# Gates of the first chunk ahead of the value products, and the second chunk's weights in halves

## The chip, the cores and the metric

The kernel runs on one core of a Trainium2 chip. The time is device time in microseconds of one launch; the median of several runs counts. The profile and the trace come from one further execution, whose times are given from the start of its span. Engines are named as in the profile: PE (TensorE), DVE (VectorE), ACT (ScalarE), POOL (GpSimd), SP (SyncE, which only issues transfers).

## What is computed

A memory attention over 8 batches, 8 heads, 576 positions and 64 columns, followed by a gated feed-forward block.

```python
a = softmax(phi, axis=memory)                     # phi: 8, 8, 576, 32
k_m = einsum('bhsm,bhsd->bhmd', a, k)             # 32 memory rows per head
v_m = einsum('bhsm,bhsd->bhmd', a, v)
attn = softmax(q @ k_m.T / sqrt(64))              # 8, 8, 576, 32
x = (attn @ v_m), heads side by side              # 4608 x 512
g, val = x @ w_gate, x @ w_val                    # 512 x 1536 each
out = (silu(g) * val) @ w_out                     # 1536 x 512
```

## The kernel before

**The product that is folded.** The kernel never forms x. For each batch it multiplies the value memories with the two weight matrices first (`u_round`, products `p_u`, line 531): U = v_m x W, 256 memory rows (8 heads of 32) by 1536 columns, for the gate (`which` 0) and the value weights (`which` 1). The gate and the value of a batch then come from U and the attention weights (`gv_half`, line 592). U lives in tiles of one chunk of 512 columns (`NCH` = 3 chunks, c = 0, 1, 2) and two groups g of memory rows; one half chunk is 256 columns (`HC`).

**Slots.** A chunk of one batch has 8 slots: four blocks of 128 columns times two halves of 288 tokens. Slot s of batch b belongs to chunk s // 8, and within a chunk slots 0 to 3 need only the first half chunk. A slot is `gv_gate`: two matmuls into a bank `p_g`, and SiLU on ACT (line 609) into `t_sg`; and later a function `mul`, kept in the list `pend`: two matmuls into a bank `p_v` and one DVE multiplication (line 615) into `t_h`. `flush_mul(n)` runs the n oldest of the list; `gv_slot` does a gate and then runs what was waiting before it, so gates run one slot ahead of values.

**Copies.** Each `p_u` bank is copied, scaled by the softmax denominator, into `t_U` by ACT ("a", line 560) or DVE ("v", line 564), as the string `evac` says, group 0 first. `later` holds back the last copy of a round, so that the caller can place it further on. `u_half` makes a round of one half chunk, for the gate weights (0,), the value weights (1,) or both (0, 1); `u_item` makes a round of a whole chunk, with the gate and the value weights in banks of their own (16 matmuls of 512 columns, 4 copies).

**Banks.** There are 8 PSUM banks. `bank` takes the one at the head of the list `free`, `done` puts it at the end, both in the order of the program text: a bank comes round again after the others, and its next writer waits until its last reader is through.

**Transfers.** The inputs are cast while they are loaded, on POOL's queue, in program order. `load_w(which, c, half)` loads a weight chunk; with a half it loads 256 columns into one half of a tile laid out as [half, row block, column], else 512 columns into [row block, column]. `w_part` gives the matmul its piece of either layout. In the head of the program the order on POOL is: keys and queries of batches 0 and 1, values, then gate and value weights of chunk 0 by halves, of chunk 1 and of chunk 2 whole; then the multiplication `norm(1, 1, nc.gpsimd)` (line 512), and behind it the output weights (`load_wo`), and the keys, phi and values of batch 2. From the ninth transfer on, each issue on POOL ends a wait for an earlier transfer.

**The head.** Everything around the change is written out by hand, from `warm(104)` (matmuls on constants that fill TensorE while the first loads come in) to the last `flush_mul()` before the list `backlog`. Batches 0 and 1 are done together: attention weights first (`scores`, `z_inv`, `norm`), then the value memories of each (`v_direct`), then slots of both in turn (`g0`, `g1`), while the first half chunk, the second half chunk, chunk 1 and chunk 2 of U are made just ahead of the slots that need them. When a chunk of slots is complete, `chunk_done` lets POOL or DVE form sums of `t_h` for the output products (line 814), which follow from 54 us on. Batch 2 begins there too (`q_T`, line 438, transposes its queries on TensorE).

Of the kernel before, what the change touches and what calls it, by code (L numbers as in the profile page):

```python
# [14 lines left out]
def kernel(  # L15
# [34 lines left out]
    NCH = DF // CH  # L50
# [24 lines left out]
    def bank(shape, dtype, name):  # L75
        tag = free.pop(0)
        t = ps.tile(shape, dtype, tag=tag, name=name)
        held[id(t)] = tag, t
        return t

    def done(*tiles):

        for t in tiles:
            free.append(held.pop(id(t))[0])
# [19 lines left out]
    def load_v(b):  # L104
        t = kvs[b]
        if b in counted:
            out = t[:, NP + 1:2 * NP + 1][:, ::-1]
        else:
            out = t[:, NP:2 * NP]
        nc.gpsimd.dma_start(out=out, in_=head_pairs(v[b]))  # L110
# [32 lines left out]
    HC = CH // 2  # L143

    def load_w(which, c, half=None):

        src = (moe_w_gate, moe_w_val)[which]
        split = half is not None
        if not half:
            W[which, c] = wpool.tile(  # L150
                [128, 2, NP, HC] if split else [128, NP, CH], BF16,
                tag=f"W{which}{c}", name=f"W{which}{c}",
            )
        f0, n = (half * HC, HC) if split else (0, CH)
        nc.gpsimd.dma_start(  # L155
            out=W[which, c][:, half] if split else W[which, c],
            in_=src[:, c * CH + f0:c * CH + f0 + n].rearrange("(i p) f -> p i f", p=128),
        )

    def w_part(which, c, i, g, halves):  # L160

        w = W[which, c][64 * g:64 * g + 64]
        h0, h1 = halves[0], halves[-1] + 1
        return w[:, h0:h1, i] if c == 0 else w[:, i, HC * h0:HC * h1]

    WO, WOc, Ts = {}, {}, {}

    def load_wo(c):
        t = wpool.tile([128, 4, DM], BF16, tag=f"WO{c}", name=f"WO{c}")
        nc.gpsimd.dma_start(  # L170
            out=t,
            in_=moe_w_out[c * CH:(c + 1) * CH, :].rearrange("(i p) f -> p i f", p=128),
        )
        for i in range(4):
            WO[4 * c + i] = t[:, i]
        WOc[c] = t
# [333 lines left out]
    def norm(b, g, eng=nc.vector):  # L510
        a = att.tile([128, 2, HALF], BF16, tag=f"A{g}", name="t_A")
        eng.tensor_tensor(out=a, in0=es.pop((b, g)), in1=lzs.pop((b, g)), op=ALU.mult)
        atts[b, g] = a
# [6 lines left out]
    def u_round(b, parts, evac, later=None, sums=None):  # L520


        banks, jobs = [], {x: [] for x in TILES}
        for which, c, halves in parts:
            w0, w1, h0, h1 = which[0], which[-1] + 1, halves[0], halves[-1] + 1
            n = (h1 - h0) * HC
            p = [bank([128, CH], FP32, f"p_u{g}") for g in range(NG)]

            def one(w, i, g, p=p, n=n, w0=w0, c=c, halves=halves):
                o = (w - w0) * n  # L530
                nc.tensor.matmul(  # L531
                    p[g][32 * i:32 * i + 32, o:o + n],
                    lhsT=kTs[b][64 * g:64 * g + 64, 2, 32 * i:32 * i + 32],
                    rhs=w_part(w, c, i, g, halves),
                    start=True,
                    stop=True,
                    tile_position=(64 * g, 32 * i),
                )

            for w in which:  # L540
                for x in TILES:
                    if sums:
                        jobs[x].append(lambda w=w, x=x, f=one: f(w, *x))
                    else:
                        one(w, *x)
            for g in range(NG):
                if (b, c, g) not in Us:
                    u_buffer(b, c, f"U{c}")
                if len(which) == 1:
                    dst = Us[b, c, g][:, h0:h1, w0]  # L550
                else:
                    dst = Us[b, c, g][:, h0]
                src = p[g][:, 0:(w1 - w0) * n].rearrange("p (a f) -> p a f", f=HC)
                banks.append((dst, src, p[g], rSs[b][:, g:g + 1] if b in scaled else None))
        def out(t, p, home, r, e):
            if e == "a":
                if r is None:
                    nc.scalar.copy(out=t, in_=p)  # L558
                else:
                    nc.scalar.activation(out=t, in_=p, func=AF.Copy, scale=r)  # L560
            elif r is None:
                nc.vector.tensor_copy(out=t, in_=p)  # L562
            else:
                nc.vector.tensor_scalar(out=t, in0=p, scalar1=r, scalar2=None, op0=ALU.mult)
            done(home)

        if sums:
            sums(jobs)
            order = (0, 2, 1, 3) if len(banks) == 4 else (0, 1, 2, 4, 3, 5)
            banks = [banks[n] for n in order]  # L570
        copies = [lambda x=x, e=e: out(*x, e) for x, e in zip(banks, evac)]
        if sums:
            return copies
        if later is not None:
            later.append(copies.pop())
        run(copies)
# [5 lines left out]
    def flush_mul(n=None):  # L582
        for _ in range(len(pend) if n is None else n):
            pend.pop(0)()

    def gv_half(b, s, which):

        jf, r = s // 2, s % 2
        c, o = jf // 4, jf % 4
        p = bank([128, CH], FP32, f"p_{'gv'[which]}")  # L590
        for g in range(NG):
            nc.tensor.matmul(  # L592
                p[:, 0:HALF],
                lhsT=Us[b, c, g][:, o // 2, which, 128 * (o % 2):128 * (o % 2 + 1)],
                rhs=atts[b, g][:, r],
                start=(g == 0),
                stop=(g == NG - 1),
            )
        return p

    def gv_gate(b, s):

        jf, r = s // 2, s % 2
        c, o = jf // 4, jf % 4
        if o == 0 and r == 0:
            hts[b, c] = hpool.tile([128, 4, S], BF16, tag=f"h{c}", name="t_h")
        gate = gv_half(b, s, 0)
        sg = work.tile([128, HALF], BF16, tag="sg", bufs=8, name="t_sg")
        nc.scalar.activation(out=sg, in_=gate[:, 0:HALF], func=AF.Silu)  # L609
        done(gate)  # L610
        dst = hts[b, c][:, o, r * HALF:(r + 1) * HALF]

        def mul():
            val = gv_half(b, s, 1)
            nc.vector.tensor_tensor(out=dst, in0=sg, in1=val[:, 0:HALF], op=ALU.mult)  # L615
            done(val)
            if o == 3 and r == 1:
                chunk_done(b, c)

        pend.append(mul)  # L620
# [7 lines left out]
    def u_buffer(b, c, tag):  # L628

        t = upool.tile([128, NG, 2, 2, HC], BF16, tag=tag, name="t_U")  # L630
        for g in range(NG):
            Us[b, c, g] = t[:, g]
# [301 lines left out]
    def u_item(b, c, evac="avav"):  # L934

        return lambda: u_round(b, (((0,), c, (0, 1)), ((1,), c, (0, 1))), evac)

    def u_half(b, which, c, half, evac):

        return lambda: u_round(b, ((which, c, (half,)),), evac)  # L940
# [18 lines left out]
    def run(items):  # L959
        for x in items:  # L960
            x()
# [13 lines left out]
    def gv_slots(b):  # L975
        return [lambda s=s: gv_slot(b, s) for s in range(2 * NJF)]
# [36 lines left out]
    load_q(1)  # L1013
    load_v(0)
    load_v(1)
    for half in range(2):
        for which in range(2):
            load_w(which, 0, half)
    for c in range(1, NCH):
        for which in range(2):  # L1020
            load_w(which, c)
    for c in range(NCH):
        u_buffer(1, c, f"S{c}")

# [25 lines left out]
    z_inv(1, 1)  # L1050
    norm(1, 0)
    norm(1, 1, nc.gpsimd)
    load_wo(0)
    load_k(2)
    nc.gpsimd.memset(kvs[2][:, NP], 1.0)
# [9 lines left out]
    g0, g1 = gv_slots(0), gv_slots(1)  # L1065
    nc.scalar.preload_act_table_set("silu_and_others")
    last_copy = []
    run([u_half(b, (0,), 0, 0, "va") for b in range(2)] + [u_half(0, (1,), 0, 0, "va")])
    u_round(1, (((1,), 0, (0,)),), "vv", last_copy)
    for s in range(4):  # L1070
        gv_gate(0, s)
    run(last_copy)
    flush_mul(2)
    for s in range(2):
        gv_gate(1, s)
        flush_mul(1)
    last_copy = []
    run([u_half(0, (0, 1), 0, 1, "va")])
    u_round(1, (((0, 1), 0, (1,)),), "av", last_copy)
    flush_mul(1)  # L1080
    run(last_copy)
    flush_mul(1)
    run(g1[2:4] + g0[4:8] + g1[4:6])
    for c in range(1, NCH):
        s = 8 * c
        run([u_item(0, c)] + g1[s - (2 if c == 1 else 3):s] + g0[s:s + 5])
        run([u_item(1, c)] + g0[s + 5:s + 8] + g1[s:s + 5])
    run(g1[-3:])
    flush_mul()
    backlog = []  # L1090

# [158 lines left out]
```

## Time and profile before

| | us |
|---|---|
| median of 3 runs (lowest, highest) | 231.17 (231.09, 231.43) |
| the profiled execution, its span | 231.35, 229.6 |
| busy: PE, DVE, ACT, POOL | 221.1, 186.6, 171.2, 151.8 |
| first product with U weights; first gate | 25.71; 27.25 |
| chunk 1's products; chunk 2's products (batch 0) | 34.64; 43.31 |
| first output products | 54.10 |

The granted clock of TensorE was 0.997 over the execution. Busy time is a union: overlapping matmuls count once. A line of the timeline merges instructions of one kind that follow each other; its second number runs from the first one's start to the last one's end, and what stands in brackets is the idle time of the engine before it and what ended it.

### The profile page before, as it was taken

Reading aid. Unit: us, or ns where it says so; the run is one execution under the profiler, and the core shown is the slowest. Engines: PE = TensorE matmul, PEld = TensorE weight load, DVE = VectorE, ACT = ScalarE, POOL = GpSimd, SP = SyncE. Lnnn points to the kernel's source line nnn. Section 1 sums busy time; section 2 is a strip of 40 time slices with the busy share of each in tenths; the row PEclk is TensorE's granted clock in tenths of the full one; section 3 lists DMA queues with packets and bytes.
Section 4 is the critical chain, followed back from the end, with each engine's and each line's share of the span. In section 5 each row is a group of like instructions: output and inputs, shape, how many; then the busy total and the mean of one; then the engine's idle time right before and its main releaser. Section 6 shows DMA issues by size and latency. Waiting matters only on the chain.

```text
span 229.6 us, 7220 instructions
## 1 busy us (share of the span) xinstructions
PE 221.1 (96%) x2826; PEld 171.3 (75%) x2826; DVE 186.6 (81%) x425; ACT 171.2 (75%) x365; POOL 151.8 (66%) x207
## 2 busy tenths in 40 slices
PE   6986899999999999999999999999999999999993
PEld 2553576778887877888788887888788878878893
DVE  4156799999977999998997768998999899977832
ACT  2867988988446899988885758978898889677311
POOL 8422736999099759979986789467545764029291
PEclk9999999999999999999999999999999999999998
DMA  6999999999995998998199945995013502202024
GB/s 207 213 211 205 198 207 207 211 256 267 207 175 135 236 276 168 223 201 205 62 227 197 204 149 120 252 226 100 32 62 113 107 0 96 91 0 94 23 92 163
DMA packets 36546, 36.84 MB, mean 160 GB/s; under 512 B 14496, under 2 KB 30880, under 8 KB 36512
## 3 DMA queue, kind: packets, MB, share of 16 engines
q0 software_dynamic: 16272, 22.42, 52.9%
q1 hardware_dynamic: 19568, 13.24, 21.6%
q10 hardware_dynamic: 672, 0.72, 0.9%
q8 instruction: 22, 0.36, 0.6%
q14 instruction: 12, 0.10, 0.1%
HBM read 42.47 MB, written 9.44 MB: 226 GB/s over the span
## 4 chain that ended last, share of the span: by engine, by line
PE 87%; DMA 9%; POOL 2%; issue 0%; ACT 0%; POOLq 0%; ACTq 0%
PE p_g L592 21%; PE p_v L592 21%; PE p_os L814 20%; PE p_oc L814 10%; DMA W<-in_moe_w_val_dram 9%; PE p_oa L814 5%; PE p_u L531 5%; PE p_kv L248 2%; PE p_os L802 1%; PE p_g L451 1%; POOL t_kv L101 1%; POOL t_kv L110 1%; POOL t_q L125 0%; PE p_q L438 0%; POOL W L155 0%
## 5 line engine op out<-in xcount | busy, mean ns | idle before, releaser
L615 DVE TENSOR_TENSOR t_h<-t_sg,p_v 128x288 bf16<-128x288 bf16 x192 | 82.1, 451 | 12.5 <-PE p_v L592 6.6
L592 PEld LDWEIGHTS <-t_U 128*128 128x128 bf16 x768 | 74.0, 98 | 20.2 <-issue 2.7
L609 ACT ACTIVATE t_sg<-p_g 128x288 bf16<-128x288 f32 x192 | 74.3, 420 | 17.8 <-PE p_g L592 11.1
L592 PE MATMUL p_g<-t_A,t_U 128*128 128x288 bf16 x384 | 77.0, 286 | 0.0
L592 PE MATMUL p_v<-t_A,t_U 128*128 128x288 bf16 x384 | 77.0, 286 | 0.0
L814 PEld LDWEIGHTS <-t_S 128*128 128x128 bf16 x384 | 37.3, 98 | 4.6 <-issue 0.2
L680 POOL TENSOR_TENSOR t_S<-t_h 128x512 bf16<-128x512 bf16 x17 | 19.6, 1154 | 21.0 <-DVE t_h L615 19.7
L814 PEld LDWEIGHTS <-t_h 128*128 128x128 bf16 x288 | 27.0, 98 | 7.3 <-issue 3.5
L558 ACT CAST t_U<-p_u 128x512 bf16<-128x512 f32 x50 | 26.4, 608 | 4.8 <-PE p_u L531 4.8
L814 PE MATMUL p_os<-t_T,t_S 128*128 128x256 bf16 x192 | 23.7, 273 | 0.0
L637 POOL TENSOR_TENSOR t_S<-t_S,t_h 128x512 bf16<-128x512 bf16 x17 | 19.6, 1155 | 1.3
L637 POOL TENSOR_TENSOR t_S<-t_h 128x512 bf16<-128x512 bf16 x16 | 18.4, 1152 | 0.0
L637 POOL TENSOR_TENSOR t_S<-t_h,t_S 128x512 bf16<-128x512 bf16 x16 | 18.4, 1151 | 0.0
L531 PE MATMUL p_u<-W,t_kT 64*32 64x512 bf16 (+1 forms) x416 | 16.8, 363 | 0.5 <-DMA W<-in_moe_w_val_dram 0.4
L562 DVE CAST t_U<-p_u 128x512 bf16<-128x512 f32 x22 | 14.3, 684 | 1.5 <-PE p_u L531 1.4
L986 PE MATMUL p_warm<-bones 128*128 128x512 bf16 x44 | 13.2, 439 | 1.7 <-DVE bones L1008 1.7
L814 PE MATMUL p_os<-t_T,t_h 128*128 128x256 bf16 x96 | 14.8, 274 | 0.0
L392 ACT COPY t_q<-p_os 128x512 f32<-128x512 f32 (+2 forms) x12 | 5.5, 469 | 9.2 <-PE p_os L802 5.1
L814 PE MATMUL p_oc<-t_T,t_S 128*128 128x256 bf16 x96 | 12.1, 273 | 0.0
L814 PE MATMUL p_oa<-WO,t_h 128*128 128x256 bf16 x96 | 11.8, 273 | 0.0
L814 PE MATMUL p_oc<-WO,t_S 128*128 128x256 bf16 x96 | 11.8, 273 | 0.0
L814 PE MATMUL p_os<-WO,t_h 128*128 128x256 bf16 x96 | 11.8, 273 | 0.0
(115 smaller groups left out, 329.6 us busy)
## 6 DMA issues: line engine op xcount, KB each, us to landing
out_dram<-t_o SPq DMA_DIRECT2D x11, 512.0 KB, 3.1
t_kv<-in_k_dram POOLq DMA_DIRECT2D x8, 576.0 KB, 10.6
t_q<-in_q_dram POOLq DMA_DIRECT2D x8, 576.0 KB, 8.3
t_kv<-in_v_dram POOLq DMA_DIRECT2D x8, 576.0 KB, 15.6
t_phi<-in_phi_dram POOLq DMA_DIRECT2D x6, 576.0 KB, 8.2
out_dram<-t_o SPq DMA_DIRECT2D x10, 256.0 KB, 8.0
WO<-in_moe_w_out_dram POOLq DMA_DIRECT2D x3, 512.0 KB, 19.0
W<-in_moe_w_gate_dram POOLq DMA_DIRECT2D x2, 512.0 KB, 16.1
```

The lines of the kernel that those rows point to most:

```text
L248: nc.tensor.matmul(p[g][32 * i:32 * i + 32, 0:n], lhsT=phi_of(b, g, j, i), rhs=kv_of(b, slice(64 * g, 64 * g + 64), w0, w1, i, j), start=( ...
L392: nc.scalar.copy(out=out, in_=in_)
L531: nc.tensor.matmul(p[g][32 * i:32 * i + 32, o:o + n], lhsT=kTs[b][64 * g:64 * g + 64, 2, 32 * i:32 * i + 32], rhs=w_part(w, c, i, g, halve ...
L558: nc.scalar.copy(out=t, in_=p)
L562: nc.vector.tensor_copy(out=t, in_=p)
L592: nc.tensor.matmul(p[:, 0:HALF], lhsT=Us[b, c, g][:, o // 2, which, 128 * (o % 2):128 * (o % 2 + 1)], rhs=atts[b, g][:, r], start=(g == 0) ...
L609: nc.scalar.activation(out=sg, in_=gate[:, 0:HALF], func=AF.Silu)
L615: nc.vector.tensor_tensor(out=dst, in0=sg, in1=val[:, 0:HALF], op=ALU.mult)
L637: eng.tensor_tensor(out=out, in0=x, in1=y, op=ALU.subtract)
L680: eng.tensor_tensor(out=t[:, 0], in0=A21, in1=A22, op=ALU.add)
L814: nc.tensor.matmul(mine[home][:, u], lhsT=lhs(c, m, u), rhs=rhs(c, m), start=fresh and u == 0, stop=(k == 5), skip_group_check=u == 1 or n ...
L986: nc.tensor.matmul(p[:, 0:128 * a], lhsT=bones, rhs=x.to_broadcast([128, a, 128]) if a > 1 else bones, start=True, stop=True,)
```

## The change

Four edits. The gates of batch 0's first four slots are placed ahead of the products with the value weights, which are then copied by DVE twice for batch 0, and by DVE and ACT for batch 1. The gates of batch 1's slots 2 and 3 are placed ahead of the second half chunk's products, with two values each time behind them. The weights of chunk 1 are loaded by halves (four transfers for two), and its products are made in two rounds, each of one half chunk for both batches. The loads of chunk 2's weights move behind `norm(1, 1, nc.gpsimd)`.

```diff
@@ w_part
-        return w[:, h0:h1, i] if c == 0 else w[:, i, HC * h0:HC * h1]
+        return w[:, h0:h1, i] if c < 2 else w[:, i, HC * h0:HC * h1]
@@ loads
-    for half in range(2):
-        for which in range(2):
-            load_w(which, 0, half)
-    for c in range(1, NCH):
-        for which in range(2):
-            load_w(which, c)
+    for c in range(2):
+        for half in range(2):
+            for which in range(2):
+                load_w(which, c, half)
@@
     norm(1, 1, nc.gpsimd)
+    for which in range(2):
+        load_w(which, 2)
     load_wo(0)
@@
-    run([u_half(b, (0,), 0, 0, "va") for b in range(2)] + [u_half(0, (1,), 0, 0, "va")])
-    u_round(1, (((1,), 0, (0,)),), "vv", last_copy)
+    run([u_half(b, (0,), 0, 0, "va") for b in range(2)])
     for s in range(4):
         gv_gate(0, s)
+    u_half(0, (1,), 0, 0, "vv")()
+    u_round(1, (((1,), 0, (0,)),), "va", last_copy)
+    for s in range(2):
+        gv_gate(1, s)
+    flush_mul(2)
     run(last_copy)
-    flush_mul(2)
-    for s in range(2):
+    for s in range(2, 4):
         gv_gate(1, s)
         flush_mul(1)
     last_copy = []
     run([u_half(0, (0, 1), 0, 1, "va")])
     u_round(1, (((0, 1), 0, (1,)),), "av", last_copy)
-    flush_mul(1)
+    flush_mul(2)
     run(last_copy)
-    flush_mul(1)
-    run(g1[2:4] + g0[4:8] + g1[4:6])
-    for c in range(1, NCH):
-        s = 8 * c
-        run([u_item(0, c)] + g1[s - (2 if c == 1 else 3):s] + g0[s:s + 5])
-        run([u_item(1, c)] + g0[s + 5:s + 8] + g1[s:s + 5])
-    run(g1[-3:])
+    flush_mul(2)
+    run(g0[4:8] + g1[4:6])
+    for half, slots in enumerate((g1[6:8] + g0[8:12] + g1[8:9], g1[9:12] + g0[12:16] + g1[12:13])):
+        run([u_half(b, (0, 1), 1, half, "av") for b in range(2)] + slots)
+    run([u_item(0, 2)] + g1[13:16] + g0[16:21])
+    run([u_item(1, 2)] + g0[21:] + g1[16:])
     flush_mul()
```

## The prediction

> **What bounds the kernel now.** I read the page first, for the engine that carries the chain, then the waits of that engine, then its timeline where it waits, then the engines that feed it there, and last the transfers. The page: busy time of TensorE, and the chain that ended last, by engine.
>
> ```profile
> PE 221.1 (96%) x2826; PEld 171.3 (75%) x2826; DVE 186.6 (81%) x425; ACT 171.2 (75%) x365; POOL 151.8 (66%) x207
> ...
> PE 87%; DMA 9%; POOL 2%; issue 0%; ACT 0%; POOLq 0%; ACTq 0%
> ```
>
> The chain is TensorE but for its head, where a transfer of value weights is waited for. So nearly every microsecond that TensorE idles or gains behind that head reaches the end. The waits of PE (us in total, times, longest) name the places:
>
> ```profile
> PE p_mT L380 <- DMA t_kv<-in_v_dram: 0.6, 1, 0.6
> PE p_u L531 <- DMA W<-in_moe_w_val_dram: 0.4, 1, 0.4
> ```
>
> The second is what the change is built around. PE's timeline there (start, length, line, operation, count):
>
> ```profile
> 25.05 0.60 PE L986 MATMUL p_warm<-bones 128*128 128x512 bf16 x2
> 25.71 0.78 PE L531 MATMUL p_u<-W,t_kT 64*32 64x256 bf16 x16
> 26.91 0.41 PE L531 MATMUL p_u<-W,t_kT 64*32 64x256 bf16 x16 [0.42 <-DMA W<-in_moe_w_val_dram]
> 27.25 1.16 PE L592 MATMUL p_g<-t_A,t_U 128*128 128x288 bf16 x8
> 28.24 0.65 PE L592 MATMUL p_v<-t_A,t_U 128*128 128x288 bf16 x4
> ...
> 29.80 0.63 PE L531 MATMUL p_u<-W,t_kT 64*32 64x256 bf16 x32
> ...
> 34.64 0.62 PE L531 MATMUL p_u<-W,t_kT 64*32 64x512 bf16 x16
> ```
>
> Gate products of both batches end at 26.49, PE idles 0.42 us, value products run from 26.91 to 27.25, then the gates. From 27.25 to 54 no wait of PE is listed: 0.42 us is all that this change can win in this stage. The helpers, ScalarE and then VectorE:
>
> ```profile
> 25.20 1.28 ACT L1066 ACT_TABLE_LOAD   x1
> 26.50 1.28 ACT L560 ACTIVATE t_U<-p_u,t_rS 128x256 bf16<-128x256 f32 x3
> 27.71 1.32 ACT L609 ACTIVATE t_sg<-p_g 128x288 bf16<-128x288 f32 x4
> ```
>
> ```profile
> 26.17 0.87 DVE L564 TENSOR_SCALAR t_U<-p_u,t_rS 128x256 bf16<-128x256 f32 x2
> 27.27 1.27 DVE L564 TENSOR_SCALAR t_U<-p_u,t_rS 128x256 bf16<-128x256 f32 x3 [0.23 <-PE p_u L531]
> 28.76 1.67 DVE L615 TENSOR_TENSOR t_h<-t_sg,p_v 128x288 bf16<-128x288 bf16 x4 [0.22 <-ACT t_sg L609]
> ...
> 32.04 3.23 DVE L615 TENSOR_TENSOR t_h<-t_sg,p_v 128x288 bf16<-128x288 bf16 x8
> 35.19 1.40 DVE L564 TENSOR_SCALAR t_U<-p_u,t_rS 128x512 bf16<-128x512 f32 x2
> ```
>
> The reader is to see two things. ScalarE's first copy of a gate product begins at 26.50 because its table load ends there. And VectorE, once it starts at 27.27, idles 0.22 us up to 35.19: it is the second engine that is nearly full.
>
> **The gates moved ahead.** They need both copies of batch 0's gate product. Single copies, in narrow windows, take 0.48 on VectorE (26.17 to 26.65) and 0.47 on ScalarE (26.50 to 26.97). A product follows a VectorE copy by 0.06 us (last copy of t_kT ends 26.14, products of batch 1 start 26.20). So the first gate's first matmul starts at 26.71 and its second at 27.03; six more at 0.1225 us (a pair each 0.245 in the timeline) end at 27.89. Idle so far: 26.49 to 26.71, 0.22, and 26.83 to 27.03, 0.20: 0.42, exactly the wait that is removed. The move alone wins nothing, since the gates wait for ScalarE about as long as the products waited for the weights.
>
> **The value products behind them.** Going from gates to u products costs 0.08 (pair at 29.47, free at 29.72, products at 29.80), and this passage is one more than before. Value products 27.97 to 28.31 (0.34 as at 26.91), weights landed long since. Then gates 0 and 1 of batch 1 (four matmuls, 0.49) to 28.80. Then the first value half, which needs batch 0's value copies. The diff puts both on VectorE ("vv"), where before one went to each engine. VectorE's first copy came 0.36 behind the products' start (26.91, 27.27), the next 0.40 later: 28.33 to 28.81 and 28.73 to 29.20. Matmuls at 28.87 and 29.26: idle 0.07 and 0.27, together 0.34. Before, the four gates lay between products and value halves as cover of 0.99 us (28.24 less 27.25); now two gates, 0.49 us, do. Behind the waiting matmul stand all of PE's later ones. Sum so far: 0.42 + 0.08 + 0.34 less 0.42 = +0.42 us.
>
> **VectorE behind.** Its idle time was 0.23 at 27.04 and 0.22 at 28.54; now it has nothing from 27.04 to 28.33, 1.29 us, so its work starts 0.84 us later for the same list: 3 copies, 13 multiplications, 2 copies up to the second chunk (four muls, one, eight: 13 in both orders). Muls back to back start 0.365 apart (32.04, 32.40, 32.77, 33.13, 33.49, 33.86); the last two, 34.33 and 34.82, were waiting for PE, so some 0.23 us is slack. Followed through the eight banks, which go round in order of release: muls 0 to 3 at 29.60 to 31.19, a half-1 copy to 31.85, two muls, the late copy to 33.24, then muls (1,2) and (1,3) to 33.97. PE wants the bank of (1,3) for a gate at 33.96, and the mul's own 0.45 us ends at 34.05 (0.365 is only the step). With the bank before it some 0.13 us of PE wait; bounds: 0 if the late copy slips ahead by one place, 0.42 (0.84 less 0.42) if all of VectorE's delay passes on. I take 0.13, the step-by-step value. The second chunk's products then start near 35.2 instead of 34.64. Afterwards VectorE's two copies and eight muls need 1.32 + 8 x 0.365 = 4.24 against 4.58 of PE: it recovers.
>
> **Edits that I cost at nothing.** Second chunk by halves: 32 products of 256 columns take what 16 of 512 take (29.80 to 30.37, 0.57; 34.64 to 35.20, 0.56), four 128x512 copies per round in both forms, and two or three slots still cover them. Without that cover a copy of 0.74 us would show. The earlier gates (1,2) and (1,3) only change places. Queues: POOL may have eight transfers out, since from the ninth on each issue waits for the eighth before it (9.67 us, 12.49, ...). The first 14 issues keep their times; multiplication norm(1,1) on POOL stays at 25.27, as the fourteenth issue still ends there. Behind it come the third chunk's two issues, then the output weights, keys and phi, all moved by two places but in the same order, and the queue holds some 15 us of work, so their landings stay. POOL's chunk sums start at 36.93 with PE, not with loads.
>
> **Landings.** Issue plus time to landing gives each arrival:
>
> ```profile
> W<-in_moe_w_gate_dram POOLq DMA_DIRECT2D x1, 512.0 KB, 16.7
> ...
> t_q<-in_q_dram POOLq DMA_DIRECT2D x1, 576.0 KB, 16.7
> ```
>
> The first, issued 15.32, lands 32.02; the second (42.64) lands 59.34, and the transposes of that tile start at 59.44: a cover of 0.10 us. Halves landed at 25.51, 26.84, 28.27, 29.59 (mean 1.36, a pair 2.72), whole tiles at 32.02, 34.57, 37.16, 39.79 (mean step 2.55). Two splits: 2 x 0.17 = 0.34 us; bounds 0 and, with every half at the longest step and every whole tile at the shortest, 4 x 1.43 - 2 x 2.43 = 0.86. I take the mean: the q tile lands at 59.68 while PE comes at 59.44 + 0.55 = 59.99: hidden, just. If PE were not later, up to 0.5 would show. Of the second chunk, the first halves land by 32.4 and the second ones by 35.0, needed at 35.2 and 39.3; the third chunk by 40.4, needed at 43.9.
>
> The Trainium skill's DMA: Bandwidth & Descriptors (Bandwidth, Measured) speaks against splitting: batch to 1 MiB or more; its 64 KB and 1 MB times, 0.95 and 6.15 us, leave an estimated 0.6 us fixed per transfer, so 1.2 us for two, and the sum by it would be 232.25. The trace, with 0.17 per split in a full queue, does not bear that out.
>
> **Sum.** 0.42 + 0.13 = +0.55 us. The profiled execution took 231.35 (span 229.6 and 1.75 around it), 0.18 over the median; 231.90 on its scale, **231.7** on the median 231.17. About 0.2%, 0.46 us, is what a measurement can tell from no change here.
>
> **The rivals.** *Value copies don't hold PE*: if VectorE's copies end before 28.80, 0.34 and 0.13 vanish and +0.08 remains, 231.25; if the gates' own idle of 0.42 goes too, -0.34, 230.8. Decisive point: gates starting by 26.5 and value products by 27.5. Against it: the table load ending 26.48. For it: every step is a few hundredths from a row. This one is not slower. *VectorE sets the pace*: its 0.84 us passes on whole, 232.0; decided by whether the 0.34 us of slack in each later round is real. For it: 5.89 of 6 us busy from 34 to 40. *Transfers late*: at the upper bound of 0.86 the q tile lands at 60.20, 0.21 behind PE, 231.95; decided at a queue delay of 0.65 us (59.99 less 59.34). For it: the cover of 0.10 is the least of these landings; against it: half tiles at 1.36. The rule of the Trainium skill named above is this rival's, with its own estimate.
>
> **How the numbers follow.** Forecast 0.50 (231.4 to 231.95, two thirds of it beyond 231.63), first rival 0.30 (a sixth of it beyond -0.46), second 0.12, third 0.08. Slower: 0.33 + 0.11 + 0.08 = 0.52; faster 0.05; same 0.43. Range 230.95 to 232.2: it leaves out the lowest part of the first rival, and of the others what lies above their prices.
>
> **What would show it.** In the profile after: no PE wait on the value weights; first gate at 26.7, second matmul held by a ScalarE copy to 27.0; value products at 28.0; a wait of 0.3 on t_U by VectorE near 29; an idle VectorE from 27.0 to 28.3; second-chunk products at 35.2. Gates at 26.5, or value halves with no wait, would prove it wrong.

## The result, and the profile after

The changed kernel takes 232.38 us in the median of 6 runs (231.86 to 232.80), the kernel before 231.11 on the same chip (231.00 to 231.43): ratio 1.0053, interval 1.0042 to 1.0063. It is slower by 1.27 us. Where single executions of a run took over 1.5% longer than its fastest (among them two of six in e11_move_qT), medians and ratios here are those of the others. The profiled execution took 232.61 us, its span 230.8. The page of the kernel after: span, PE's row, the instruction queue of the transfers, and the chain that ended last.

```profile
span 230.8 us, 7286 instructions
...
PE 221.6 (96%) x2858; PEld 171.1 (74%) x2858; DVE 186.3 (81%) x425; ACT 171.5 (74%) x365; POOL 153.3 (66%) x209
...
q8 instruction: 22, 0.36, 0.6%
...
PE 88%; DMA 7%; POOL 1%; issue 1%; DVE 1%; ACT 0%; POOLq 0%; ACTq 0%
```

PE has 32 more products and 32 more weight loads (2858 for 2826 in each), so 64 more instructions. "issue", time in which the engine waited for nothing that the profile shows, has 1% of the chain where it had 0%; that share is rounded and alone says little, but the waits of PE in the kernel after name a place:

```profile
PE p_os L814 <- issue: 0.7, 1, 0.7
...
PE p_g L592 <- ACT t_U L560: 0.5, 1, 0.5
```

The wait for the value weights is gone. In its place stands one of about the same length (0.5 for 0.4) for ACT's copies of U, and a wait that was nowhere before: 0.7 us on nothing. First the head, PE's timeline of the kernel after (start, length, line, operation, count):

```profile
25.74 0.41 PE L531 MATMUL p_u<-W,t_kT 64*32 64x256 bf16 x16 [0.59 <-DVE t_kT L394]
26.64 1.16 PE L592 MATMUL p_g<-t_A,t_U 128*128 128x288 bf16 x8 [0.49 <-ACT t_U L560]
27.73 0.41 PE L531 MATMUL p_u<-W,t_kT 64*32 64x256 bf16 x16
28.07 0.66 PE L592 MATMUL p_g<-t_A,t_U 128*128 128x288 bf16 x4
28.64 0.93 PE L592 MATMUL p_v<-t_A,t_U 128*128 128x288 bf16 x4
...
30.48 0.63 PE L531 MATMUL p_u<-W,t_kT 64*32 64x256 bf16 x32
...
35.01 0.63 PE L531 MATMUL p_u<-W,t_kT 64*32 64x256 bf16 x32
```

The gates wait to 26.64. The first value halves stretch: four matmuls, then the next one at 29.41, 0.77 us where four in a row take 0.49. DVE's timeline of the same kernel shows why:

```profile
28.10 1.27 DVE L564 TENSOR_SCALAR t_U<-p_u,t_rS 128x256 bf16<-128x256 f32 x3 [1.12 <-PE p_u L531]
29.44 1.67 DVE L615 TENSOR_TENSOR t_h<-t_sg,p_v 128x288 bf16<-128x288 bf16 x4
31.03 0.75 DVE L564 TENSOR_SCALAR t_U<-p_u,t_rS 128x512 bf16<-128x512 f32 x1
...
33.08 2.63 DVE L615 TENSOR_TENSOR t_h<-t_sg,p_v 128x288 bf16<-128x288 bf16 x7
35.63 1.40 DVE L564 TENSOR_SCALAR t_U<-p_u,t_rS 128x512 bf16<-128x512 f32 x2
```

DVE idles 1.12 us, and from 28.10 to the second chunk's copies at 35.63 it has no bracket left: 7.53 us without a gap. Now the place of the new wait, a hundred microseconds behind the change: the timeline of all engines in the kernel after.

```profile
132.44 0.38 PE L814 MATMUL p_os<-t_T,t_Q 128*128 128x256 bf16 x2
...
132.91 0.41 PE L592 MATMUL p_v<-t_A,t_U 128*128 128x288 bf16 x2
...
133.98 0.60 PE L814 MATMUL p_os<-t_T,t_Q 128*128 128x256 bf16 x4 [0.67 <-issue]
133.98 0.42 PEld L814 LDWEIGHTS <-t_Q 128*128 128x128 bf16 x4 [0.85 <-issue]
```

These matmuls read tiles of the same names as the two at 132.44, which had run. PE's timeline of the kernel before has no wait there:

```profile
131.98 0.38 PE L814 MATMUL p_os<-t_T,t_Q 128*128 128x256 bf16 x2
...
132.44 0.41 PE L592 MATMUL p_v<-t_A,t_U 128*128 128x288 bf16 x2
132.69 0.60 PE L814 MATMUL p_os<-t_T,t_Q 128*128 128x256 bf16 x4
```

From the value matmuls to the output products it takes 0.25 us there and 1.07 in the kernel after, so 0.82 are lost; the profile's 0.67 counts only from the modelled end of the matmul before. Followed through both traces (first start of each, us):

| | before | after | difference |
|---|---|---|---|
| first half chunk's second products | 29.80 | 30.48 | +0.68, of which 0.49 are gates moved ahead |
| second chunk's products | 34.64 | 35.01 | +0.37 |
| first output products | 54.10 | 54.48 | +0.38 |
| first output products on t_Q, batch 4's turn | 131.98 | 132.44 | +0.46 |
| last matmul | 225.81 | 227.06 | +1.25 |

So a part of the loss arises in the head and a larger one, 0.79, behind 132 us, where the wait's 0.82 accounts for it. The head was forecast, the other place was not.

### The profile page after: what moved, and what is told of

Its sections match the earlier page's. It is cut to its first block, busy times and chain, and to the rows that moved or that the text cites. A ratio compares the mean times of both kernels' runs of the same rounds, so it can differ in the third digit from the quotient of the medians.

```text
span 230.8 us, 7286 instructions
## 1 busy us (share of the span) xinstructions
PE 221.6 (96%) x2858; PEld 171.1 (74%) x2858; DVE 186.3 (81%) x425; ACT 171.5 (74%) x365; POOL 153.3 (66%) x209
## 4 chain that ended last, share of the span: by engine, by line
PE 88%; DMA 7%; POOL 1%; issue 1%; DVE 1%; ACT 0%; POOLq 0%; ACTq 0%
PE p_g L592 21%; PE p_v L592 20%; PE p_os L814 20%; PE p_oc L814 10%; DMA t_kv<-in_v_dram 7%; PE p_oa L814 5%; PE p_u L531 5%; PE p_kv L248 2%; PE p_os L802 1%; PE p_g L451 1%; POOL t_kv L101 1%; PE p_mT L380 1%; PE p_warm L986 1%; POOL t_q L125 0%; PE p_q L438 0%
```

## The experiments

Three theories were tested; where the expectations use letters, A is the first, D and E are the two forms of the second (copies that hold PE; VectorE's pace), F is the third, and B, C and G are rivals stated with them. **Instruction blocks:** the 64 more PE instructions move the places at which the instruction stream is refilled, and one refill comes late. Its evidence: q8 moves 22 packets of 16 KB (0.36 MB) for some 5,700 PE instructions (matmuls and weight loads), about 260 each. **Head:** the new order costs some 0.5 us by itself, by copies that hold PE, or because DVE's list sets the pace. **Transposes:** the refill is late because it stands behind the query transposes on the transfer engines (SP's `DMA_TRANSPOSE t_qT`, 123.70 to 130.89 in the kernel after).

### The two parts one at a time

**e2_whole**: the change, with the second chunk's products whole as before (its loads still by halves).

```diff
-    for half, slots in enumerate((g1[6:8] + g0[8:12] + g1[8:9], g1[9:12] + g0[12:16] + g1[12:13])):
-        run([u_half(b, (0, 1), 1, half, "av") for b in range(2)] + slots)
-    run([u_item(0, 2)] + g1[13:16] + g0[16:21])
-    run([u_item(1, 2)] + g0[21:] + g1[16:])
+    for c in range(1, NCH):
+        s = 8 * c
+        run([u_item(0, c)] + g1[s - (2 if c == 1 else 3):s] + g0[s:s + 5])
+        run([u_item(1, c)] + g0[s + 5:s + 8] + g1[s:s + 5])
+    run(g1[-3:])
```

> The changed kernel with the second chunk's products as before (whole chunk per batch, 16 matmuls of 512 columns); its weights still come in halves, the head is still reordered. PE has as many instructions as in the kernel before. Theory A: no wait for issue near 133; what is left is the stage loss of the head, 0.35 to 0.55 us over the kernel before. Rival B: as slow as the changed kernel, 1.2 to 1.3 us over the kernel before.

Measured: 231.85 us, ratio 1.0032 (1.0020 to 1.0044), +0.68 on 231.17. Its profile has no wait for "issue"; its second chunk comes at 35.04, its last matmul at 226.20, 0.86 before that of the change.

**e3_head_undone**: the change, with the order of the head as before.

```diff
-    run([u_half(b, (0,), 0, 0, "va") for b in range(2)])
+    run([u_half(b, (0,), 0, 0, "va") for b in range(2)] + [u_half(0, (1,), 0, 0, "va")])
+    u_round(1, (((1,), 0, (0,)),), "vv", last_copy)
     for s in range(4):
         gv_gate(0, s)
-    u_half(0, (1,), 0, 0, "vv")()
-    u_round(1, (((1,), 0, (0,)),), "va", last_copy)
+    run(last_copy)
+    flush_mul(2)
     for s in range(2):
-        gv_gate(1, s)
-    flush_mul(2)
-    run(last_copy)
-    for s in range(2, 4):
         gv_gate(1, s)
         flush_mul(1)
...
-    flush_mul(2)
+    flush_mul(1)
     run(last_copy)
-    flush_mul(2)
-    run(g0[4:8] + g1[4:6])
+    flush_mul(1)
+    run(g1[2:4] + g0[4:8] + g1[4:6])
```

> The changed kernel with the head's old order (value products ahead of the gates, the old copies); second chunk's weights and products still by halves, third chunk's loads still moved. Theory A: the stage loss is gone (second chunk's products at 34.6 to 34.7, as before) but the wait for issue near 133 stays, so 0.5 to 0.9 us over the kernel before. Rival B, with the loss in the head: the same time as the kernel before; with the loss in the transfers: the output products late from 54 us on.

Measured: 231.67 us, ratio 1.0030 (1.0015 to 1.0044), with a spread from 231.19 to 232.85 where the kernel before has 231.00 to 231.43. The second chunk's products come at 34.49, 0.55 before those of e2_whole. The timelines of PE at that place, first of e2_whole, then of e3_head_undone:

```profile
35.04 0.62 PE L531 MATMUL p_u<-W,t_kT 64*32 64x512 bf16 x16
```

```profile
34.49 0.63 PE L531 MATMUL p_u<-W,t_kT 64*32 64x256 bf16 x32
```

The 32 products by halves take what 16 whole ones take (0.63 and 0.62), as the prediction had it. But the waits of PE in e3_head_undone hold the new wait, without any change of the head:

```profile
PE p_os L814 <- issue: 0.3, 1, 0.3
```

So the two parts cost about 0.68 and 0.50, 1.18 together, of the 1.27 seen.

### Is it the number of instructions?

**e1_before_rows**: the kernel before, its first fillers cut into narrow ones, so that PE has 64 more instructions and the same work.

```diff
-    warm(104)
+    warm(88, 47)
```

> The kernel before with nothing changed but its first filler, warm(104) written as warm(88, 47): 58 constant matmuls in place of 26, so PE's stream has 64 instructions more (32 weight loads, 32 matmuls), as many as the second chunk by halves adds, and the same stage work, copies and transfers. Theory A (instruction blocks: the page has 22 instruction packets of 16 KB for some 5,700 PE instructions, 260 each; the idle 0.67 us at 133.98 of the changed kernel is the next block arriving late behind the DMA transposes of 123.70 to 130.89): the wait for issue near 133 appears here as well, 0.4 to 0.9 us, and the time is 0.4 to 0.9 us over the kernel before. Rival B (the loss comes from the reordered gates, copies and transfers alone, and the idle at 133.98 belongs to that one profile): no such wait, the same time within 0.1 us.

Measured: 231.61 us, ratio 1.0025 (1.0010 to 1.0039). The profiled execution has no wait for "issue" and took 233.31 for another reason, seen in its windows (from:to, length, busy time and instructions of PE, PEld, DVE, ACT, POOL, granted clock, DMA share, GB/s):

```profile
0.00:20.00 20.00, 16.22 (x212) 10.93 (x213) 7.12 (x28) 10.92 (x16) 9.38 (x18) 0.78 1.02 210
20.00:25.00 5.00, 4.67 (x79) 2.89 (x78) 3.15 (x8) 2.99 (x8) 1.18 (x2) 0.86 1.31 202
```

In this execution the granted clock fell to 0.78, and its first U product came at 27.47. Ten of the twelve executions had a mean clock of 0.993 or more and took 231.22 to 231.76, so the median's +0.44 is not the clock's; but no trace of one of them was kept, so it does not tell whether the wait was there: inconclusive.

**e4_after_rows**: the same edit on the changed kernel, so 128 more instructions than before.

> The changed kernel with the first filler as warm(88, 47): 64 PE instructions more than the changed kernel, 128 more than the kernel before. Theory A: the place in PE's stream where the block runs out is reached 64 instructions (some 3.5 us) earlier, near 129.5, while the transposes still hold the next block back until about 131.4 (it served PE at 133.98): a wait of 3 to 5 us, and a time 3 to 5 us over the changed kernel, unless the block is asked for before the transposes begin, in which case the wait is gone and the time is 0.7 us under the changed kernel. Rival B: the same time as the changed kernel within 0.2 us.

Measured: 232.28 us, ratio 1.0051 (1.0038 to 1.0064), as the change itself. The wait of 3 to 5 us that the theory gave did not come, so its forecast failed in size. The wait at 133 is gone, and one stands at 82, where the kernel before and the change have none; PE's timeline of e4_after_rows:

```profile
81.65 0.40 PE L592 MATMUL p_g<-t_A,t_U 128*128 128x288 bf16 x2
82.36 0.42 PE L592 MATMUL p_v<-t_A,t_U 128*128 128x288 bf16 x2 [0.31 <-DVE t_bkv L305]
```

The profile names DVE's `t_bkv`, which these matmuls do not read. With matmuls and weight loads counted together in the order of their starts, this gap (0.59 us from one start to the next) stands behind PE's 2,230th instruction; the wait of the change and of e3_head_undone stands behind the 3,509th in both. To within one place the distance is 1,280, five times 256.

**e5_before_tiny32**: the kernel before with 32 tiny matmuls on constants (64 x 32, 64 columns, into the next free bank, which is put back at once) in an idle stretch of the head: again 64 more instructions, and nothing of the change.

```diff
     warm(12)
+    tiny(32)
     run(q1)
```

> The kernel before plus 32 small matmuls on constants (64x32 by 64 columns, results unused) just before the transposes of batch 1's queries, where PE idles 1.15 us for a transfer: 64 PE instructions more, nothing else moved, the fillers that hold the clock untouched. Theory A (the 257th instruction of a block waits when its block is late; the wait for issue sat behind PE's instruction 3509 in the changed kernel and in the one with the old head, and behind instruction 2230, five blocks of 256 earlier to one, in the changed kernel with 64 more): as in the kernel with the old head, a wait for issue behind instruction 3509 near 133 us in part of the executions, median 0.2 to 0.6 us over the kernel before and a spread of over 1 us. Rival C (the halved products or loads themselves cost the time, in the second chunk or in the transfers): the time and the spread of the kernel before, within 0.1 us.

Measured: 231.58 us, ratio 1.0024 (1.0003 to 1.0044), from 231.07 to 233.39: the times of the kernel before (beside it 231.02 to 231.31, and one of 232.18) and up to 2 us more. The waits of PE in e5_before_tiny32:

```profile
PE p_u L531 <- DMA W<-in_moe_w_val_dram: 0.5, 1, 0.5
PE p_os L814 <- issue: 0.5, 1, 0.5
```

The first is the wait of the kernel before. The second is the new one, behind instruction 3,509 again, at a granted clock of 1.0. Nothing of the change is in this kernel: the number of instructions puts the wait there.

**e6_head_tiny96** and **e7_after_tiny96**: e3_head_undone and the change with 96 tiny matmuls, so 256 instructions, four times 64, more than before. The aim was to bring the refills back to their old places.

```diff
     warm(12)
+    tiny(48)
     run(q1)
...
     scores(1, 1)
+    tiny(48)
     v_direct(0, "vvvv")
```

> The kernel with the old head and the second chunk by halves (231.67, spread 1.66 us) plus 96 of the small matmuls, 48 at each of two places where PE idles for a transfer: 256 PE instructions more than the kernel before, exactly one block, so the block ends fall on the same work as before. Theory A: no wait for issue behind the scores of batch 5, median within 0.2 us of the kernel before and a spread of some 0.5 us. Rival C: as the kernel with the old head, 0.5 us over the kernel before with the wide spread, or slower for the added matmuls.

> The changed kernel plus the same 96 small matmuls, 256 PE instructions more than the kernel before. Theory A: only the head's own loss is left, 0.55 to 0.75 us over the kernel before as with whole products (231.85), no wait for issue. Rival C: as slow as the changed kernel, 1.2 us over the kernel before.

Measured: 234.26 us (ratio 1.0093, 1.0055 to 1.0131) and 235.13 us (1.0172, 1.0150 to 1.0194). The first is a median of two sorts: three executions at a mean clock of 0.999 or 1.0 took 231.89 to 232.27, five at 0.985 to 0.993 took 234.24 to 235.02, the profiled one among them. No wait near 133 is left, but both have one in the head. The waits of PE in e6_head_tiny96:

```profile
PE p_g L478 <- issue: 1.9, 1, 1.9
...
PE p_tiny L1001 <- issue: 0.3, 1, 0.3
```

In e7_after_tiny96 the first is 2.1 and the second not listed. The long one stands behind instruction 697 in both, three past 694, and 3,510 less 694 is eleven times 256; the short one stands behind 442, four past 438, another 256 earlier. The granted clock fell as well, to 0.70 (e6_head_tiny96, 20 to 28 us) and 0.80 (e7_after_tiny96). The experiment moved the wait to a worse place and can't give the times without it.

### Why PE has to wait for the refill

The packets of the instruction queue in the trace, against PE's stream:

| | packet starts, ends | PE could go on at | from the start | PE waited |
|---|---|---|---|---|
| after | 131.37, 132.55 | 133.98 | 2.61 | 0.67 |
| e3_head_undone | 130.64, 131.82 | 133.14 | 2.50 | 0.35 |
| e5_before_tiny32 | 130.78, 131.97 | 133.35 | 2.57 | 0.51 |
| e4_after_rows | 79.88, 80.90 | 82.36 | 2.48 | 0.31 |

In all four PE goes on 2.5 to 2.6 us after the packet's start. In e1_before_rows the packet starts at 131.26 and PE comes to the 3,510th instruction at 134.67, 3.4 us later: no wait. The same interval accounts for the run without the wait. It also holds elsewhere: counted in order, the packets stand one for one ahead of instructions 182, 182 + 256 and so on, 3,510 among them (22 packets, and 23 in the two runs with 256 instructions more). In the 13 traces, behind the head (from 60 us on), PE comes to none of these places sooner than in the four rows above; the next is 2.65 us, without a listed wait.

The traces also show what the count changes. Instructions 3,254 and 3,510 are two such places. In the five traces with the old count (the kernel before, e2_whole, e8_cover, e9_cover_a1, e10_cover_a2) PE takes 8.2 us from one to the other, and the packet starts 3.7 to 4.7 us behind the first. With 64 instructions more other work lies between the two, and PE runs it in 5.8 us where it does not wait (e1_before_rows, e11_move_qT). In the three that wait there the packet starts 3.8 to 4.0 us behind the first place, no later than with the old count, but 2.5 us more are then too many; in the two that do not it starts 2.4 and 1.8 us behind. So it is PE that comes sooner, not the packet that comes later. The wait of e4_after_rows has the same form (3.2 us behind its place, in a stretch of 5.7 us, wait included), and no transpose runs near it. SP's timeline of e4_after_rows:

```profile
61.68 5.92 SPq L134 DMA_TRANSPOSE t_qT<-t_q  x1
67.66 32.92 SPq L760 DMA_DIRECT2D out_dram<-t_o  x9
100.68 6.91 SPq L134 DMA_TRANSPOSE t_qT<-t_q  x1
```

So a transpose is not needed for such a wait. Whether the transposes delay the packet at 3,510 is what the next run tries.

**e11_move_qT**: e3_head_undone, with batch 5's query transposes issued at the head of batch 4's turn, 10 us earlier.

```diff
+            if b == 4:
+                load_qT(5)
             run(take(6))
...
-            if b > 2:
+            if b > 2 and b != 4:
                 load_qT(b + 1)
```

> The kernel with the old head and the second chunk by halves (231.67, spread 1.66 us), with the DMA transposes of batch 5's queries issued at the head of batch 4's turn, some 10 us sooner, instead of behind it. Theory F (the block that PE lacks behind instruction 3509 is late because the transposes from 123.2 to 130.7 are in its way): no wait for issue there, median within 0.2 us of the kernel before, spread under 0.6 us. Rival G (it is late for another reason): the same median and spread as the kernel with the old head, a wait behind instruction 3509.

Measured: 233.11 us, ratio 1.0082 (1.0069 to 1.0095): slower. The transposes run from 113.31 to 118.19, the packet starts at 128.60, 2.04 us earlier than in e3_head_undone, PE comes to the 3,510th instruction at 132.54, 3.9 us after that, and there is no wait. But PE's waits in e11_move_qT have another, of U's products for the key transposes of batch 5:

```profile
PE p_u L531 <- DMA t_kT<-t_bkv: 1.7, 1, 1.7
```

Its median is therefore no test. In its one trace, with the transposes away, the packet came earlier and the wait went, as the theory has it. Against it stand e1_before_rows and e4_after_rows, where the packet for 3,510 started in the middle of the transposes (131.26 in 125.23 to 133.84; 125.71 in 124.30 to 130.76), 2.4 and 1.5 us behind its place, and the wait of e4_after_rows at 82 without any. What fixes the moment at which a packet is sent stays open.

### The head: copies that hold PE, or DVE's pace?

**e8_cover**: e2_whole, with all four gates of batch 1 ahead of the first value half, as cover for the value copies.

```diff
-    for s in range(2):
+    for s in range(4):
         gv_gate(1, s)
     flush_mul(2)
     run(last_copy)
-    for s in range(2, 4):
-        gv_gate(1, s)
-        flush_mul(1)
+    flush_mul(2)
```

> The kernel with the reordered head and whole products (231.85) with all four gates of batch 1 ahead of the first value half, then two value halves, the late copy and two more: 0.98 us of gates cover the value copies in place of 0.49. Theory D (the value copies on VectorE hold PE): the wait of 0.3 on t_U before the first value half goes, the second chunk's products start near 34.7 in place of 35.04, 231.4 to 231.6. Rival E (VectorE's late start sets the pace, its 3 copies, 13 multiplications and 2 copies follow without a gap): PE wins the wait and gives it back at the banks, second chunk's copies on VectorE not earlier, 231.75 to 231.9.

Measured: 231.93 us, ratio 1.0030 (1.0021 to 1.0039): nothing won. From the first product to the second half's products it takes 4.39 us (26.04 to 30.43), in e2_whole 4.74 (25.78 to 30.52), so 0.35 are won there. To the second chunk it takes 9.28 (to 35.32) and 9.26 (to 35.04): all of it is given back. DVE's timeline in e8_cover, then PE's where the time is given back:

```profile
28.39 1.27 DVE L564 TENSOR_SCALAR t_U<-p_u,t_rS 128x256 bf16<-128x256 f32 x3 [1.12 <-PE p_u L531]
...
35.94 1.40 DVE L564 TENSOR_SCALAR t_U<-p_u,t_rS 128x512 bf16<-128x512 f32 x2
```

```profile
33.13 0.41 PE L592 MATMUL p_v<-t_A,t_U 128*128 128x288 bf16 x2
33.53 0.42 PE L592 MATMUL p_g<-t_A,t_U 128*128 128x288 bf16 x2
33.89 0.41 PE L592 MATMUL p_v<-t_A,t_U 128*128 128x288 bf16 x2
34.25 0.40 PE L592 MATMUL p_g<-t_A,t_U 128*128 128x288 bf16 x2
```

7.55 us for the same list (0.22 of it idle), 7.53 in e2_whole and in the change. With the copies covered, PE loses the time further on: its pairs start 0.36 to 0.40 us apart where 0.245 is their own pace, about the 0.365 at which DVE's multiplications, which free the banks, follow each other. That it is the banks that PE waits for is read from this pace; the profile lists no wait there.

**e9_cover_a1** takes one 128x512 copy off that list (to ACT); **e10_cover_a2** one 128x256 copy more.

```diff
     run([u_half(0, (0, 1), 0, 1, "va")])
-    u_round(1, (((0, 1), 0, (1,)),), "av", last_copy)
+    u_round(1, (((0, 1), 0, (1,)),), "aa", last_copy)
```

```diff
-    u_half(0, (1,), 0, 0, "vv")()
+    u_half(0, (1,), 0, 0, "va")()
```

> The kernel with four gates of batch 1 as cover (231.93), and one copy of the half-1 round of batch 1, 128x512, moved from VectorE to ScalarE. Theory E (VectorE's list from its first value copy to the second chunk's copies takes 7.53 us without a gap in the changed kernel, 7.53 with whole products and 7.55 with more cover, whatever PE's order): the list gets 0.66 us shorter, the second chunk's products start 0.4 to 0.66 us sooner after the first ones, the median falls to 231.3 to 231.6. Rival D (the matmuls' own waits for the copies): ScalarE's later copy holds the gates that need it, median 231.9 or over.

> As the last, and the second value copy of batch 0 on ScalarE as well (another 0.4 us off VectorE's list). Theory E: VectorE is no longer the last, PE's own order is (some 34.5 for the second chunk's products with a first product at 25.78); 231.2 to 231.4, not under the kernel before by more than 0.1 us, since the gates still wait for ScalarE's copies behind its table load or for the first weights. Rival D: no change from the last one, or slower as SiLU waits behind the copy.

Measured: 231.49 us, ratio 1.0008 (0.9998 to 1.0017), and 231.51 us, ratio 1.0007 (0.9998 to 1.0015), against 231.24: no difference from the kernel before can be told. DVE's timeline in e9_cover_a1:

```profile
28.38 1.27 DVE L564 TENSOR_SCALAR t_U<-p_u,t_rS 128x256 bf16<-128x256 f32 x3 [1.31 <-PE p_u L531]
...
35.48 1.40 DVE L564 TENSOR_SCALAR t_U<-p_u,t_rS 128x512 bf16<-128x512 f32 x2
```

7.10 us, 0.45 less than in e8_cover, with the same 0.22 idle. From the value products to the second chunk PE takes 6.92 us (28.01 to 34.93), in e8_cover 7.30 (28.02 to 35.32): 0.38 won. Against the kernel before, measured beside each, the median went from +0.76 to +0.25, by 0.51. The second copy wins nothing more (27.99 to 34.91, again 6.92): there DVE idles 0.61 us, PE's pairs follow each other by 0.245 from 32.12 on, and PE's own order sets the pace. The gates stand first in both, so the move of the gates wins nothing even with a lighter DVE. None of the versions tried beats the kernel before.

## Why the prediction was wrong

**Direction right, size less than half.** The forecast was +0.55 us, all of it in the head; +1.27 came, and 232.38 lies above the range.

**The step that failed** is "Edits that I cost at nothing", its first sentence: the second chunk by halves. That 32 products of 256 columns take what 16 of 512 take is right. But they are 32 more matmuls and 32 more weight loads, and that was not counted. e5_before_tiny32 shows that 64 more instructions, without any of the change, put a wait behind instruction 3,509, and e3_head_undone, the halves without the new head, has it too: +0.41 and +0.50 us in the medians. The 64 instructions put other work between two of the places at which the stream is refilled, work that PE would run in 5.8 us where it had 8.2, and the packet does not come that much sooner. No rival held this case, and none of the signs listed would have shown it: they all lie before 36 us.

**The gates moved ahead: right.** Gates at 26.64 (forecast 26.71), held by ScalarE's copies, idle 0.49 us for the 0.42 of the removed wait. They wait in one piece instead of two. ScalarE's table load ends at 25.98 here and was not what held them; the products were already 0.37 us shorter (0.41 for 0.78), since PE had waited 0.59 us for the last copy of the value memories and had both batches' when it began.

**The value products behind them: right in size.** Value products at 27.73 (27.97), value halves at 28.64, which is 0.08 behind the gates' own pace (28.87 and 0.07), then 0.28 lost in their four matmuls (0.27).

**VectorE behind: right size, wrong term.** The forecast let 0.42 pass by way of PE's own order and 0.13 by way of the banks. The head cost 0.55 us by the second chunk's products in e2_whole and e3_head_undone (0.64 from their own first products, 25.78 and 25.87), and 0.68 in the median of e2_whole. But the 0.34 of the value copies is not what sets it: e8_cover removed 0.35 there and got nothing, as DVE's list of 7.5 us then ended no earlier. e9_cover_a1 shortened the list by 0.45 and got 0.38 up to the second chunk, 0.51 in the median. So the mechanism is that of the second rival, *VectorE sets the pace*, at less than its price of 0.84.

**A direct comparison of the two traces hides part of this.** It shows +0.37 at the second chunk. The profiled execution of before was slow there: its value weights let PE start at 26.91, those of e5_before_tiny32, with the same order, at 26.63, and its second chunk came at 34.64, not 34.36.

**Landings: right.** The query tile lands at 58.72 (43.02 and 15.7) with PE at 59.82, so the third rival did not occur (its price, 231.7 and 0.21, is 231.9 rather than 231.95). The two splits cost 5.29 less 4.98, 0.31 us, from the value weights' last half of the first chunk (29.39, before 29.59) to the end of the second chunk (34.68, before 34.57); forecast 0.34. The 0.6 us per added transfer estimated from the Trainium skill's DMA: Bandwidth & Descriptors (Bandwidth, Measured) is not borne out in this full queue.

**Not accounted for:** between the first output products at 54 us and 132 us the change loses another 0.08, and the parts add up to 1.18 of 1.27 us; both are below what these runs can tell. With one trace of each run it also stays open how far the wait accounts for the spread of the medians' executions.

## What to carry to other kernels

Cost an edit in instructions of each engine as well as in time: here work that takes the same time in twice as many instructions moved every later refill of the stream, and the price appeared 100 us behind the edit; a few idle matmuls in the old kernel show whether it is that. Before covering a wait of one engine, follow the list of the engine that feeds it: here that list had next to no gap, so that cover won nothing and only a shorter list did. Where a reorder removes a wait, read what the moved work itself waits for at its new place: here 0.49 us for 0.42.

## What the runs showed of the hardware

- PE stood still behind instructions that lie, to within four places, multiples of 256 apart (3,509, 2,230, 697 and 442), for 0.3 to 2.1 us, with a 16 KB packet of the instruction queue just before. It went on 2.5 to 2.6 us after that packet's start at the first two, 2.2 to 2.4 us after it in the head (e6_head_tiny96: 21.66 and 23.91, 15.57 and 17.98; e7_after_tiny96: 22.25 and 24.51). The profile calls it "issue", or (e4_after_rows) names an engine whose tile these matmuls do not read.
- The programs with the wait at 3,509 spread more: 231.07 to 233.39 us in e5_before_tiny32, 231.19 to 232.85 in e3_head_undone, where the kernel before, measured beside them, took 231.02 to 231.31 (and one of 232.18) and 231.00 to 231.43.
- Fillers of 128 columns and tiny ones in the head went with a granted clock of 0.78 (e1_before_rows, 0 to 20 us) and 0.70 (e6_head_tiny96, 20 to 28 us) in the profiled executions. The same fillers went with 1.0 in e4_after_rows (0 to 20 us), and 32 tiny ones with 1.0 in e5_before_tiny32. So these runs do not show that the fillers lower it.
